# Token order of the last block, and stores of 32 rows, in a linear-attention and softplus-MLP kernel

## The chip, the cores and the metric

The kernel runs on one core of a Trainium2 chip. The core has a matrix engine (TensorE, PE; its weight loads are shown apart as PEld), a vector engine (VectorE, DVE), a scalar engine (ScalarE, ACT), a general engine (GpSimd, POOL) and a synchronisation engine (SyncE, SP), which in this kernel issues all the large DMAs. The metric is the time on the device for one execution, in microseconds (us). A profile is one execution; its span runs from the first to the last instruction.

## What is computed

Two blocks follow each other. The first is a linear attention with a normalised output, for 8 batches of 8 heads, 576 tokens and 64 features:

```python
kv = einsum('bhsd,bhse->bhde', k, v)
o  = einsum('bhsd,bhde->bhse', q, kv)
x  = o / sqrt(mean(o*o, axis=-1) + 1e-6) * g_norm
```

Its result is turned into 4608 tokens of 512 features, and the second block is

```python
h   = x @ w_in            # 512 -> 2048
out = softplus(h) @ w_out # 2048 -> 512
```

The result is 4608 rows of 512 float32 numbers, a row being 2 KB.

## The kernel before

**Tiles, blocks and phases.** The tokens are cut into 36 tiles of 128 (P), t = 0 to 35, and these into 12 blocks of three tiles (TB = 3), n = 0 to 11. The 2048 hidden features are 16 chunks of 128. One step is one chunk for one block: 12 matmuls of w_in against the block's x (L658, 384 tokens wide), softplus on ACT (L678), a split of its result into three terms that together keep the precision (L680 on ACT, L669 and L673 on DVE), and 9 matmuls of those against w_out (L665). The weights of all chunks don't fit, so the chunks are worked in three phases; the sums of a phase are written to DRAM (part) and added in the next (L703 loads them, L705 adds on DVE). In the last phase L705 makes the output rows in a tile ot, and a store on SP takes them to out.

**x on its way.** The attention makes x of a tile on DVE (L535), while steps of earlier blocks run on PE. The matmuls want x with features as rows, so it must be turned. Tiles 0 to 11 are turned by PE (BY_PE = 12, L540) and stored to a DRAM buffer xd[n] of 512 features by 384 tokens. From tile 12 on DVE does it in blocks of 32 x 32 (L615), into a tile xb that holds three tiles, a block's worth. The ring xb has one place. When the third tile is in, four DMAs (L619), one for each group a of 32 partitions, store it to xd[n]. In xb the 32 tokens of group a of the three tiles lie beside each other, so the stores write runs of 3 x 32 = 96 tokens (384 B), and the tokens of a block stand in xd[n] in the order (group a, tile, token in the group) and not in their own. The steps don't care for the order of tokens. x_of(t) then reads back 128 consecutive columns (L636), which are four groups of 32 tokens that come from different tiles. x_there[t] holds the stores that this load waits for.

**Results put back in order.** For tiles from 12 on the rows of a result tile are thus four groups of 32 rows, each of which belongs to another place of out. Group m of tile i of the block is group a of the original tile u, with a, u = divmod(4 * i + m, 3). The store (L711 to L719) puts neighbouring groups with the same a into one DMA, whose destination is then k runs of 32 rows that lie 128 rows apart. For i = 0, 1, 2 this gives 3 + 1, 2 + 2 and 1 + 3 groups: two DMAs for a tile. Tiles 0 to 11 are stored by one DMA of 128 rows (L723, L724).

**What sets the order.** A planner (class Plan) gets every piece of work with an engine, an estimated time in ns, what it comes after, the places of rings that it takes and gives back, a position pos, and for DMAs a size in ns. It plays the run through and issues the program in the order that comes out. On each engine that order is fixed: an instruction that waits holds all behind it. A task that needs a ring's place is put where the planner expects the place to be free; a real semaphore wait guards it on the chip. For a DMA task the place comes free at the planner's own DMA time plus 2000 ns. Result tiles come from rings m (13 places) and x (2 places).

Of the kernel before, what the change touches and what calls it, by code (L numbers as in the profile page):

```python
# [18 lines left out]
P = 128  # L19
# [21 lines left out]
class Plan:  # L41
# [13 lines left out]
    def slot(self, ring):  # L55
        return Slot(ring)

    def add(self, engine, ns, run, after=(), pos=0.0, take=(), give=(), size=0, behind=None, follows=None):
        t = Task(engine, ns, run, [a for a in after if a is not None], pos, list(take), list(give), size)
        for s in t.give:  # L60
            s.readers += 1
        self.tasks.append(t)
        t.follows = follows
        t.behind = behind
        return t
# [77 lines left out]
def kernel(  # L143
# [24 lines left out]
    nc = tc.nc  # L168
    B, H, S, D = q.shape
    d_model, d_ff = moe_w_in.shape  # L170
# [4 lines left out]
    NT = 384  # L175
    TB = NT // P
    n_blocks = n_tokens // NT
    n_tiles = n_tokens // P
# [5 lines left out]
    LAST = PHASES[-1]  # L184
# [5 lines left out]
    BY_PE = 12  # L190
# [27 lines left out]
    slot, add = plan.slot, plan.add  # L218

    def new(s, shape, dtype=F32):  # L220
        pool = ps if s.ring in PS else sb
        s.tile = pool.tile(shape, dtype, tag=f"{s.ring}_{s.place}", name=f"{s.ring}_{s.place}")
        return s.tile
# [164 lines left out]
    def parts(t):  # L388

        b, s0 = divmod(t * P, S)  # L390
        if s0 + P <= S:
            return [(b, 0, P, s0)]
        return [(b, 0, S - s0, s0), (b + 1, S - s0, P - S + s0, 0)]

    first_tile = [b * S // P for b in range(B)]
    xd = [dram.tile([d_model, NT], F32, name=f"x{n}") for n in range(n_blocks)]
# [5 lines left out]
    BL = 32  # L402
# [57 lines left out]
    def x_pos(t):  # L460

        n = t // TB
        return t * EARLY[0] + EARLY[1] if n == 0 else first_step[0, n] - (EARLY[2] if n == 1 else EARLY[3]) + t % TB
# [52 lines left out]
    def rows(t):  # L516
        pos = x_pos(t)
# [24 lines left out]
        def part_of_qT(n, r0):  # L542
            if qT.tile is None:
                new(qT, [P, NP, P])
            return qT.tile[:, :, r0:r0 + n]

        turned = []
        for b, r0, n, s0 in parts(t):
            if b >= 2:
                if b not in q_slots:  # L550
# [3 lines left out]
                        out=part_of_qT(n, r0),  # L554
                        in_=q_slots[b].tile.rearrange("k (p s) -> k p s", p=NP)[:, :, s0:s0 + n]),
# [28 lines left out]
            a = add("PE", 440, turn_q, [ld], pos - 1, [tp], [q_s])  # L584
# [3 lines left out]
        a = o_task = add("PE", 830 if len(parts(t)) == 1 else 1350, out_rows, turned + need, pos, [o], [qT])  # L588
        for pt in parts(t):
            o_tasks.setdefault(pt[0], []).append(a)  # L590
        a = add("ACT", 600, lambda: nc.scalar.activation(new(x, [P, H, D]), o.tile, func=AF.Square,  # L591
                                                              scale=D ** -0.5), [a], pos, [x])
        a = add("DVE", 690, reduce, [a], pos, [r])
        a = add("POOL", 2300, root, [a], pos)
        a = add("DVE", 700, norm, [a, o_task], pos, [], [o, r])
        if t < BY_PE:
            a = add("PE", 440, turn_x, [a], pos + 0.5, [xp], [x])
            if t < AT_ONCE:
                split(0, t, xp, a, pos + 0.5)
            a = add("ACT", 600, lambda: nc.scalar.copy(new(xg, [P, KD, P]), xp.tile), [a], pos + 1, [xg], [xp])  # L600
            x_there[t] = [add("SP", 450, lambda: nc.sync.dma_start(
                out=x_of(t), in_=xg.tile), [a], pos + 1, [], [xg], 1000)]
# [2 lines left out]


        n, i = divmod(t, TB)
        if i == 0:
            xb_slots[n] = slot("xb"), []
        xb, turns = xb_slots[n]  # L610

        def turn_blocks():
            if i == 0:
                new(xb, [P, d_model // BL, TB, BL])
            nc.vector.transpose(out=xb.tile[:, :, i], in_=x.tile.rearrange("p h d -> p (h d)").rearrange(  # L615
                "p (b j) -> p b j", j=BL))

        def store(a):
            nc.sync.dma_start(out=xd[n][:, a * TB * BL:(a + 1) * TB * BL].rearrange("(b i) m -> i b m", i=BL),  # L619
                              in_=xb.tile[a * BL:(a + 1) * BL].rearrange("i b t j -> i b (t j)"))  # L620

        turns.append(add("DVE", 710, turn_blocks, [a], pos, [] if i else [xb], [x], follows=turns[-1] if i else None))
        if i == TB - 1:
            stores = [add("SP", 450, lambda a=a: store(a), turns, pos + 0.5, [], [xb], 820) for a in range(P // BL)]
            for u in range(n * TB, t + 1):
                x_there[u] = stores

    def x_of(t):

        n, i = divmod(t, TB)  # L630
        return xd[n][:, i * P:(i + 1) * P].rearrange("(a p) t -> p a t", p=P)
# [9 lines left out]
    part = {}  # L641
# [3 lines left out]
    def step(s):  # L645
# [38 lines left out]
        for i in range(TB):  # L684
            last = c == cs[-1]
            a2 = add("PE", 700, lambda i=i: mm2(i), [a] + factors_done[1, c] + [mm2s.get(i)], s + 1.5,
                     [mine[i]] if c == cs[0] else [],
                     [gv] + ([w_out] if s == last_step[c] else []))
            mm2s[i] = a2
            if last:  # L690
                leave(ph, n * TB + i, mine[i], a2, s + 1.5)
# [3 lines left out]
    def leave(ph, t, bank, done, pos):  # L695

        ot = slot("m" if ph == 0 else ("m", "x", "m")[t % TB] if ph == LAST else "m")
        if ph == 0:
            a = add("ACT", 600, lambda: nc.scalar.activation(new(ot, [P, d_model]), bank.tile, func=AF.Copy, scale=1.0 + E),
                    [done], pos, [ot], [bank])  # L700
        else:
            pt = slot("m")
            ld = add("SP", 350, lambda: nc.sync.dma_start(out=new(pt, [P, d_model]), in_=part[ph - 1, t][0]),  # L703
                     [part[ph - 1, t][1]], pos - EARLY[10], [pt], [], 900, behind=int(pos) - 4)
            a = add("DVE", 700, lambda: nc.vector.scalar_tensor_tensor(  # L705
                out=new(ot, [P, d_model]), in0=bank.tile, scalar=(scale if ph == LAST else 1.0 + E), in1=pt.tile,
                op0=ALU.mult, op1=ALU.add), [done, ld] + (scale_done if ph == LAST else []), pos, [ot], [bank, pt])
        if ph == LAST and t >= BY_PE:
            n, i = divmod(t, TB)

            def store():  # L711
                m = 0
                while m < P // BL:
                    a, u = divmod(P // BL * i + m, TB)
                    k = min(TB - u, P // BL - m)
                    nc.sync.dma_start(
                        out=out[n * NT:(n + 1) * NT].rearrange("(t s) f -> t s f", t=TB)[u:u + k, a * BL:(a + 1) * BL],
                        in_=ot.tile[m * BL:(m + k) * BL])
                    m += k  # L719

            part[ph, t] = None, add("SP", 800, store, [a], pos, [], [ot], 750)
            return
        dst = out[t * P:(t + 1) * P] if ph == LAST else dram.tile([P, d_model], F32, name=f"part{ph}_{t}")  # L723
        st = add("SP", 350, lambda: nc.sync.dma_start(out=dst, in_=ot.tile), [a], pos, [], [ot], 720)  # L724
        part[ph, t] = dst, st
# [28 lines left out]
    for c in range(KF):  # L754
        for j in (2 * c, 2 * c + 1):
            pos = CONVERT[j] if c < 4 else LATER[c - 4] + LATER[12] * (j % 2)
            weight(j, pos, FETCH[j] if c < 4 else pos)
    for b in range(B):
        kv_of(b)
        for t in range(n_tiles):  # L760
            if parts(t)[-1][0] == b:
                rows(t)
# [51 lines left out]
```

## Time and profile before

| what | value |
|---|---|
| median of three timed runs | 934.63 us (933.73 to 934.82) |
| the profiled run, timed | 934.44 us |
| span of its profile | 932.7 us |
| DMA, mean over the span | 141 GB/s |
| stores of results, L716 | 48: 16 of 192 KB, 16 of 128 KB, 16 of 64 KB |
| stores of results, L724 to out | 12 of 256 KB |
| stores of x from xb, L619 | 32 of 192 KB |

In lines of the profile an operation is named by engine, line and operation; out<-in are the tiles that it writes and reads. The row of an issue on SP (SPq) shows only the time that issuing took, not when the data landed. In a table of stretches, each row has the stretch, its length, the busy time and number of instructions for PE, PEld, DVE, ACT and POOL, the clock granted to PE, the busy share of the 16 DMA engines and what they moved in GB/s. In the row of DMA a digit is the share of the engines that is busy in a column, in tenths.

### The profile page before, as it was taken

To read this page: it belongs to the slowest core of one execution; us is meant where nothing else is said; L and a number is where in the kernel's file an instruction comes from. 1 tells how busy PE (TensorE), PEld (TensorE's weight loads), DVE (VectorE), ACT (ScalarE), POOL (GpSimd) and SP (SyncE) were. 2 spreads that over 40 slices of the span, in tenths; PEclk is the share of its full clock that TensorE was granted. 3 is DMA by queue.
4 is the path that set the end of the run, shared out by engine and by line. 5 is a ranking of instruction groups with operands and counts; after the bars stand their busy time and mean duration, and the time that the engine had idled before them with its cause. 6 is when DMAs were issued, how large, how long until landed. Compare 5 with 4: busy or idle time off the path is not lost.

```text
span 932.7 us, 13257 instructions
## 1 busy us (share of the span) xinstructions
PE 904.9 (97%) x4821; PEld 818.5 (88%) x4821; DVE 627.3 (67%) x1055; ACT 414.5 (44%) x799; POOL 80.4 (9%) x78
## 2 busy tenths in 40 slices
PE   7899999999999999999999999999999999999992
PEld 5689899989999999999999999989999998999992
DVE  6777788776458887788757878887434455655531
ACT  4766555444433656464424455555322323333320
POOL 0323421221113100000000000000000000000000
PEclk8999999999999999999999999999999999999997
DMA  8999998498782554346334445551231233444321
GB/s 213 225 225 222 248 212 205 102 212 151 171 143 90 147 147 136 112 145 206 102 102 128 148 157 169 189 182 39 85 102 56 81 102 102 106 119 127 109 75 42
DMA packets 231377, 131.43 MB, mean 141 GB/s; under 512 B 130448, under 2 KB 205200, under 8 KB 231312
## 3 DMA queue, kind: packets, MB, share of 16 engines
q1 hardware_dynamic: 231152, 130.58, 53.3%
q8 instruction: 38, 0.62, 0.3%
q14 instruction: 27, 0.22, 0.1%
q10 hardware_dynamic: 160, 0.00, 0.0%
HBM read 91.75 MB, written 38.80 MB: 140 GB/s over the span
## 4 chain that ended last, share of the span: by engine, by line
PE 93%; SPq 2%; DVE 1%; DMA 1%; POOL 1%; ACT 1%; issue 0%; ACTq 0%
PE s L665 43%; PE h L658 43%; PE o L523 3%; PE o L506 3%; SPq L568 1%; DMA g_col<-in_g_norm_dram 1%; PE tp L540 0%; POOL r L532 0%; DMA m<-in_v_dram 0%; DMA qa<-in_q_dram 0%; DVE m L312 0%; PE tp L578 0%; DVE r L528 0%; DVE xv L440 0%; DVE m L316 0%
## 5 line engine op out<-in xcount | busy, mean ns | idle before, releaser
L658 PE MATMUL h<-xv,w 128*128 128x384 f32 x2304 | 434.6, 337 | 0.0
L665 PE MATMUL s<-w,gv 128*128 128x512 f32 x1728 | 434.3, 395 | 0.0
L658 PEld LDWEIGHTS h<-xv,w 128*128 128x128 f32 x2304 | 406.2, 188 | 14.8 <-issue 0.2
L665 PEld LDWEIGHTS s<-w,gv 128*128 128x128 f32 x1728 | 319.5, 188 | 59.1 <-issue 0.5
L678 ACT ACTIVATE g<-h 128x384 f32<-128x384 f32 x192 | 94.3, 491 | 398.4 <-PE h L658 394.4
L669 DVE TENSOR_TENSOR gv<-g,gv 128x384 fp32r<-128x384 f32 x192 | 106.6, 555 | 175.9 <-ACT gv L680 175.0
L680 ACT ACTIVATE gv<-g 128x384 fp32r<-128x384 f32 x192 | 100.9, 525 | 23.3 <-PE s L665 16.6
L673 DVE SCALAR_TENSOR_TENSOR gv<-gv 128x384 fp32r<-128x384 f32 x192 | 107.0, 557 | 6.0
L440 DVE SCALAR_TENSOR_TENSOR xv<-m,g_col,xv 128x512 fp32r<-128x512 f32 x102 | 75.8, 743 | 1.1 <-ACT xv L437 1.1
L444 DVE SCALAR_TENSOR_TENSOR xv<-xv 128x512 fp32r<-128x512 f32 x108 | 74.5, 690 | 2.6
L437 ACT ACTIVATE xv<-m,g_down 128x512 fp32r<-128x512 f32 x102 | 69.7, 710 | 2.5 <-DMA m<-x 2.4
L532 POOL TENSOR_TENSOR r<-r,half 128x8 f32<-128x8 f32 x36 | 65.8, 1826 | 3.0
L506 PEld LDWEIGHTS o<-m,m 128*128 128x128 f32 x256 | 34.2, 200 | 8.7 <-issue 7.3
L506 PE MATMUL o<-m,m 128*128 128x128 f32 x256 | 35.4, 285 | 6.4 <-DMA m<-in_v_dram 6.4
L705 DVE SCALAR_TENSOR_TENSOR m<-s,scale,m 128x512 f32<-128x512 f32 x24 | 17.9, 747 | 29.7 <-PE s L665 29.7
L523 PE MATMUL o<-kv_diag,m 128*128 128x128 f32 (+1 forms) x296 | 36.9, 275 | 0.0
L523 PEld LDWEIGHTS o<-kv_diag,m 128*128 128x128 f32 (+1 forms) x296 | 35.0, 179 | 1.8 <-issue 1.0
L531 POOL TENSOR_SCALAR r<-r 128x8 f32<-128x8 f32 x36 | 13.9, 386 | 244.9 <-DVE r L528 244.8
L535 DVE TENSOR_TENSOR x<-o,r 128x512 f32<-128x512 f32 x33 | 22.7, 688 | 17.6 <-POOL r L532 17.6
L528 DVE TENSOR_REDUCE r<-x 128x8 f32<-128x512 f32 x36 | 24.5, 681 | 13.3 <-ACT x L591 13.2
L705 DVE SCALAR_TENSOR_TENSOR m<-s,m 128x512 f32<-128x512 f32 x36 | 23.3, 684 | 10.2 <-PE s L665 10.1
L286 ACT ACTIVATE sq<-raw 128x512 bf16<-128x512 bf16 x32 | 21.3, 665 | 16.4 <-DMA raw<-in_moe_w_in_dram 10.2
(67 smaller groups left out, 445.6 us busy)
## 6 DMA issues: line engine op xcount, KB each, us to landing
m<-x SPq DMA_DIRECT2D x102, 256.0 KB
part<-m SPq DMA_DIRECT2D x72, 256.0 KB
m<-part SPq DMA_DIRECT2D x72, 256.0 KB
raw<-in_moe_w_in_dram SPq DMA_DIRECT2D x16, 512.0 KB
m<-in_k_dram SPq DMA_DIRECT2D x64, 128.0 KB
m<-in_v_dram SPq DMA_DIRECT2D x32, 256.0 KB
raw<-in_moe_w_out_dram SPq DMA_DIRECT2D x16, 512.0 KB
qa<-in_q_dram SPq DMA_DIRECT2D x24, 288.0 KB
```

The lines of the kernel that those rows point to most:

```text
L437: nc.scalar.activation(cols(0, F32R), x.tile, func=AF.Identity, scale=g_down)
L440: nc.vector.scalar_tensor_tensor(out=cols(1, F32R), in0=x.tile, scalar=g_col, in1=cols(0), op0=ALU.mult, op1=ALU.subtract)
L444: nc.vector.scalar_tensor_tensor(out=cols(2, F32R), in0=cols(1), scalar=-RADIX, in1=cols(0), op0=ALU.mult, op1=ALU.add)
L506: nc.tensor.matmul(kv[:, i if tail else p], lhsT=l, rhs=r, start=(p == 0 and i == 0), stop=tail, skip_group_check=True)
L523: nc.tensor.matmul(y[r0:r0 + n, p::NP], lhsT=qT.tile[:, p, r0:r0 + n], rhs=kv_diag[b % 2][:, p].rearrange("r (h d) -> r h d", d=D), start= ...
L532: nc.gpsimd.tensor_tensor(out=r.tile, in0=r.tile, in1=half, op=ALU.pow)
L658: nc.tensor.matmul(hp, lhsT=w_in.tile[:, i, kd * P:(kd + 1) * P], rhs=xv.tile[:, i, kd], start=(m == 0), stop=(m == 3 * KD - 1))
L665: nc.tensor.matmul(mine[i].tile, lhsT=gv.tile[:, m, i * P:(i + 1) * P], rhs=w_out.tile[:, m], start=(c == cs[0] and m == 0), stop=(c == cs ...
L669: nc.vector.tensor_tensor(out=gv.tile[:, 1], in0=g.tile, in1=gv.tile.bitcast(F32)[:, 0], op=ALU.subtract)
L673: nc.vector.scalar_tensor_tensor(out=gv.tile[:, 2], in0=f32[:, 1], scalar=-RADIX, in1=f32[:, 0], op0=ALU.mult, op1=ALU.add)
L678: a = add("ACT", 490, lambda: nc.scalar.activation(new(g, [P, NT]), h.tile, func=AF.Softplus, scale=1.0 + E), [a], s, [g], [h])
L680: a = add("ACT", 530, lambda: nc.scalar.activation(new(gv, [P, 3, NT], F32R)[:, 0], g.tile, func=AF.Copy, scale=DOWN), [a], s, [gv])
```

## The change

There are two parts.

The last block (n = 11, tiles 33, 34 and 35) keeps its tokens in order. A group size g is 3 for the other blocks and 1 for the last: each of its tiles takes an xb of its own, is turned into it, and is stored by four DMAs, whose runs are 32 tokens (128 B) instead of 96. A tile's read-back then waits for its own stores alone. As its tokens are in order, its results leave by the plain path, L723 and L724, one DMA of 128 rows for each tile.

The other tiles from 12 on (12 to 32) store their results by four DMAs of 32 rows, one for each group, whose destinations are each contiguous, in place of two whose destinations have up to three runs. The planner's time for the four is 1600 ns instead of 800, and its size for a store of the last block's x is 490 instead of 820.

```diff
         n, i = divmod(t, TB)
+        g = TB if n < n_blocks - 1 else 1
+        i0, i = i - i % g, i % g
         if i == 0:
             xb_slots[n] = slot("xb"), []
...
-                new(xb, [P, d_model // BL, TB, BL])
+                new(xb, [P, d_model // BL, g, BL])
...
-            nc.sync.dma_start(out=xd[n][:, a * TB * BL:(a + 1) * TB * BL].rearrange("(b i) m -> i b m", i=BL),
+            nc.sync.dma_start(out=xd[n][:, i0 * P + a * g * BL:i0 * P + (a + 1) * g * BL].rearrange("(b i) m -> i b m", i=BL),
...
-        if i == TB - 1:
-            stores = [add("SP", 450, lambda a=a: store(a), turns, pos + 0.5, [], [xb], 820) for a in range(P // BL)]
-            for u in range(n * TB, t + 1):
+        if i == g - 1:
+            stores = [add("SP", 450, lambda a=a: store(a), turns, pos + 0.5, [], [xb], 820 if g > 1 else 490)
+                      for a in range(P // BL)]
+            for u in range(t - i, t + 1):
                 x_there[u] = stores
...
-        if ph == LAST and t >= BY_PE:
+        if ph == LAST and BY_PE <= t < n_tiles - TB:
             n, i = divmod(t, TB)
 
             def store():
-                m = 0
-                while m < P // BL:
+                for m in range(P // BL):
                     a, u = divmod(P // BL * i + m, TB)
-                    k = min(TB - u, P // BL - m)
-                    nc.sync.dma_start(
-                        out=out[n * NT:(n + 1) * NT].rearrange("(t s) f -> t s f", t=TB)[u:u + k, a * BL:(a + 1) * BL],
-                        in_=ot.tile[m * BL:(m + k) * BL])
-                    m += k
-
-            part[ph, t] = None, add("SP", 800, store, [a], pos, [], [ot], 750)
+                    row = n * NT + u * P + a * BL
+                    nc.sync.dma_start(out=out[row:row + BL], in_=ot.tile[m * BL:(m + 1) * BL])
+
+            part[ph, t] = None, add("SP", 1600, store, [a], pos, [], [ot], 750)
             return
```

## The prediction

> **What bounds the kernel now.** I read the engine shares first, then a table of stretches, then the end of the timeline, then the DMA columns there. The page's first line:
>
> ```profile
> PE 904.9 (97%) x4821; PEld 818.5 (88%) x4821; DVE 627.3 (67%) x1055; ACT 414.5 (44%) x799; POOL 80.4 (9%) x78
> ```
>
> TensorE (PE) is the bound. A mean hides where its missing 3% lies, so the table of stretches (start:end, length, busy time of each engine, clock, DMA share, GB/s) is next:
>
> ```profile
> 0.00:50.00 50.00, 39.93 (x229) 31.58 (x230) 35.28 (x63) 30.28 (x59) 9.93 (x14) 0.93 0.87 215
> ...
> 300.00:345.00 45.00, 45.00 (x238) 41.01 (x237) 37.77 (x66) 27.10 (x55) 7.49 (x7) 1.00 0.54 149
> ...
> 771.00:896.00 125.00, 125.00 (x629) 113.35 (x628) 69.19 (x114) 40.98 (x78) 0.00 (x0) 1.00 0.38 108
> 896.00:916.30 20.30, 20.26 (x100) 17.57 (x98) 8.95 (x15) 4.47 (x9) 0.00 (x0) 1.00 0.28 78
> 916.30:932.70 16.40, 0.00 (x0) 0.00 (x0) 0.75 (x2) 0.00 (x0) 0.00 (x0) 0.59 0.21 48
> ```
>
> From 100 us to 916.3 us PE has no idle stretch: there, moving a DMA can only do harm or nothing. But 16.4 us at the end hold no matmul at all. What lies there, from the timeline (start, length):
>
> ```profile
> 914.91 0.75 DVE L705 SCALAR_TENSOR_TENSOR m<-s,scale,m 128x512 f32<-128x512 f32 x1 [0.59 <-PE s L665]
> 915.61 0.75 DVE L705 SCALAR_TENSOR_TENSOR x<-s,scale,m 128x512 f32<-128x512 f32 x1
> 915.69 1.21 SPq L716 DMA_DIRECT2D out_dram<-m  x2
> 916.30 0.75 DVE L705 SCALAR_TENSOR_TENSOR m<-s,scale,m 128x512 f32<-128x512 f32 x1
> 917.01 1.53 SPq L716 DMA_DIRECT2D out_dram<-x  x2
> 918.64 1.29 SPq L716 DMA_DIRECT2D out_dram<-m  x2
> ```
>
> The last result (tile 35) is ready at 917.05, its second store is issued by 919.93. SP's waits for the stretch from 905 us on say what follows:
>
> ```profile
> SPq L809 <- DMA out_dram<-m: 11.6, 1, 11.6
> ```
>
> The drain at L809 waits 11.6 us for the last stores. Why so long for 768 KB? The DMA columns of 912 to 933 us (40 columns of 0.525 us; tenths busy over 16 engines, then GB/s):
>
> ```profile
> DMA  1100000000492332234221111111111111100000
> GB/s 47 47 12 0 0 0 0 0 0 23 39 78 51 70 105 86 51 55 94 78 59 51 51 39 27 35 47 55 47 55 51 51 55 47 55 31 16 0 0 0
> ```
>
> The stores crawl at about 50 GB/s with a tenth of the engines busy: in 924 to 928 us the stretch reads share 0.13 and 44 GB/s, so 0.13 x 16 = 2 engines at 21 GB/s each. The last data is at column 35, about 930.6; the span ends 2.1 us later. The same 768 KB from a block whose tokens are in order (tiles 0 to 2, L724), 648 to 660 us in columns of 0.3 us:
>
> ```profile
> DMA  0000000006980009949985799999869999898651
> GB/s 0 0 0 0 0 0 0 0 0 239 348 287 0 0 0 341 375 150 348 314 285 121 205 309 295 341 336 306 258 205 239 304 278 355 335 382 341 266 198 61
> ```
>
> One 256 KB store, issued at 649.97, fills columns 9 to 11, (239 + 348 + 287) x 0.3 = 262 KB in 0.9 us, from 650.7: 16 engines.
>
> **What the Trainium skill says.** "DMA: Bandwidth & Descriptors", section "Why a DMA increments its semaphore by 16 and not by 1": the number of engines is the largest up to 16 that divides the slowest dimension, size-1 ones apart, of both access patterns. For a destination of 3 x 32 rows that is 3, for 2 x 32 rows 2, for 32 or 128 rows 16, always the lowest-numbered ones. The trace agrees: per tile L716 issues 3+1, 2+2, 1+3 groups of 32 rows, so the last three tiles give engines 0 and 1 each 64 x 4 = 256 KB and engine 2 128 KB; 256 KB at 21 GB/s is 12.5 us. The same page, "Anatomy of one DMA", gives some 2 us of fixed cost, most of it the write's receipt; the 2.1 us after the last column agree. Its "Specifications" want runs of 512 B for line rate; the trace's 384-byte runs (x<-xb, L619) go at about 170 GB/s, the q loads' 128-byte runs at about 138 GB/s with engines full, the 2 KB stores above at 350.
>
> **The change part by part.**
>
> *Last block's results (tiles 33 to 35): six L716 issues out, three L724 stores of 128 rows in.* Issue: a plain L724 store takes 0.34 us. Results are ready at 915.66, 916.36, 917.05 (DVE is untouched), so the third is issued at about 917.1; its data starts 0.75 us later (649.97 to 650.7), 917.85. The three transfers need 3 x 0.9 us from 915.69 + 0.75 = 916.45 at the earliest, so the second ends near 918.1 and the third at 919.0. With 2.1 us to the end: 921.1; with the receipt a little shorter in an idle machine, down to 920.6. I take 920.9. Against 932.7: **11.8 us saved**, all of it on the path that sets the end.
>
> *Tiles 12 to 32: four stores of 32 rows, 64 KB each, instead of two.* 42 issues become 84. Each of the old pair has a median of 0.59 to 0.74 us; the new one is two-dimensional like L724 (0.34), so a tile costs SP 1.4 us at best and 4 x 0.59 = 2.4 at worst against 1.2, for three tiles of a block of 20.9 us 0.6 to 3.6 us more. Queued behind them on SP are the loads of partial sums (L703) and of x (L636). Those of the last block are issued at 862.71 to 868.56 and first read by ACT at 879.55, so 11 us of slack hide the delay. There is a gain too that nobody waits for: L636's three loads take 5.8 us to issue behind a store on few engines, 1.5 us elsewhere. On the path: nothing, since PE is full from 771 to 916.
>
> *Last block's x (rows 33 to 35, 310 to 337 us): three times four stores of 64 KB in runs of 128 B instead of four of 192 KB in runs of 384 B.* SP: 8 issues more x 0.70 us (2.82 us per four at 331.40) = 5.6 us, into SP's idle stretches of 312.25 to 320.38 and 320.72 to 331.40; hidden. DMA: 2048 pieces of 384 B at 170 GB/s cost 4.6 us; now 6144 of 128 B, at 138 GB/s 5.7 us; were a piece as dear as a 384-byte one, 13.8 us. DMA's share there is 0.54, and the block's x is read back at 337.23 for steps that begin at 358: hidden. What is not clearly hidden is a **new wait**. Ring xb has one place, so each tile's block transpose (L615) must wait till the stores of the tile before have landed. DVE then:
>
> ```profile
> 311.93 0.71 DVE L615 STREAM_TRANSPOSE xb<-x 128x512 f32<-128x512 f32 x1
> ...
> 314.37 0.56 DVE L669 TENSOR_TENSOR gv<-g,gv 128x384 fp32r<-128x384 f32 x1 [0.55 <-ACT gv L680]
> 314.96 0.56 DVE L673 SCALAR_TENSOR_TENSOR gv<-gv 128x384 fp32r<-128x384 f32 x1
> ...
> 316.04 0.70 DVE L615 STREAM_TRANSPOSE xb<-x 128x512 f32<-128x512 f32 x1
> ```
>
> Tile 34's transpose at 316.04 moves back. Tile 33's stores can be issued from 312.7 to 315.5, behind 2 MB that the columns show flowing until 316.4. Their data (256 KB) takes 1.9 to 4.6 us, the receipt 2: landed between 318.5 (nothing ahead) and 323. The planner puts the transpose where it believes the place free, with 4 x 490 ns for these data where I have 1.9 to 4.6 us, 1.8 us of issues where the trace has 2.8, 6.96 us for the transfers ahead where it shows 7.7. So DVE may stand at it 0.7 to 4.3 us. Behind it in order stand L669 and L673, whose output PE reads 1.75 us after it is ready (315.52, the matmul at 317.27). PE can lose 0 to 2.6 us, once: tile 35 comes 14 us later. A gain is excluded, since PE is full there. I take 0.4, nearer the low end, as the planner may leave L669 ahead of the transpose.
>
> *Sum against the profiled span*: 932.7 - 11.8 + 0.4 = 921.3. The three timed runs (median 934.63) stand 1.9 us above this span: **923.2 us**.
>
> **Rivals.** (1) The forecast, 921.8 to 924.3: 0.70. (2) The tail goes, but the new wait costs PE 1.5 to 4 us: 924.3 to 926.8, at 0.14. For it: DVE is 84% busy from 300 to 345 us. Against: the planner knows the wait. (3) The tail goes only in part, say because three stores that arrive together make the write receipt slow, 3 to 6 us more: 926 to 929, at 0.06. Against it: 16 engines ran at 350 GB/s at 650 us. (4) Slower. A 128-byte write to HBM could cost far more than the 128-byte read that the trace shows. Place: tile 34's transpose, with all of DVE and then PE held behind it. Each ns of packet cost is 128 packets per engine and tile = 0.13 us; the 11.8 us are eaten once stores land some 13.5 us (with the 1.75 of slack) after the plan's 2 us of data, about 120 ns a packet, against 36 for one of 384 B. At 150 ns a tile's data takes 19 us, the loss is 15, and the time 938: 0.05. (5) The store's tail turns out to be bound by the end of the program and not by the stores, which leaves 934.6, no change: 0.05 with all other ways to nothing; the columns, which show data till 930.6, speak against it.
>
> **How the numbers follow.** A measurement tells 0.2%, 1.9 us, from no change. Faster: 0.70 + 0.14 + 0.06 = 0.90, and part of (5) makes 0.91; same 0.03; slower 0.06 with mishaps of (2) beyond its end. The low end is the forecast less 0.3 us of the receipt and 1.1 us of the spread of the runs, 921.8; the high end takes in most of (2): 926.5.
>
> **What would show it.** After the change the last columns should read 250 to 350 GB/s for 3 us, SP's final wait should fall from 11.6 to about 3.5 us, and the last matmul should still end near 916.3. A last matmul later than 918, with DVE idle before L615 near 318 us, would be (2); beyond 928, (4). It is wrong if the three stores still land at 50 GB/s.

## The result

| kernel | median, us | runs | span of its profile, us |
|---|---|---|---|
| before | 934.66 | 933.73 to 934.82, 4 | 932.7 |
| changed | 922.49 | 922.42 to 922.67, 4 | 920.4 |

The changed kernel takes 0.9871 of the time before, with an interval of 0.9855 to 0.9887: 12.2 us less, where 11.5 had been forecast (923.2 us, range 921.8 to 926.5).

**Where the time came from.** The table of stretches of the changed kernel (start:end, length, busy PE, PEld, DVE, ACT, POOL, clock, DMA share, GB/s), to be held against the one of before:

```profile
300.00:345.00 45.00, 45.00 (x238) 41.01 (x237) 37.95 (x67) 28.00 (x56) 7.74 (x7) 1.00 0.58 152
...
771.00:896.00 125.00, 125.00 (x629) 113.35 (x628) 69.45 (x114) 41.01 (x78) 0.00 (x0) 1.00 0.37 108
896.00:916.30 20.30, 20.30 (x101) 17.78 (x99) 8.69 (x15) 4.69 (x10) 0.00 (x0) 1.00 0.27 78
916.30:920.40 4.10, 0.22 (x1) 0.00 (x0) 1.01 (x2) 0.00 (x0) 0.00 (x0) 1.00 0.51 192
```

PE is as full as it was up to its last matmul. The stretch after that is 4.1 us and not 16.4, and DMA runs in it at 192 GB/s on the mean and not at 48. The timeline of the end (start, length):

```profile
915.17 0.75 DVE L708 SCALAR_TENSOR_TENSOR m<-s,scale,m 128x512 f32<-128x512 f32 x1 [0.59 <-PE s L668]
915.87 0.75 DVE L708 SCALAR_TENSOR_TENSOR x<-s,scale,m 128x512 f32<-128x512 f32 x1
915.95 0.35 SPq L723 DMA_DIRECT2D out_dram<-m  x1
916.56 0.75 DVE L708 SCALAR_TENSOR_TENSOR m<-s,scale,m 128x512 f32<-128x512 f32 x1
916.65 0.35 SPq L723 DMA_DIRECT2D out_dram<-x  x1
917.34 0.33 SPq L723 DMA_DIRECT2D out_dram<-m  x1
```

Each result is issued within 0.1 us of its end, in one DMA. SP's wait at the end, and the DMA columns of 912 to 921 us (0.225 us each):

```profile
SPq L808 <- DMA out_dram<-m: 1.7, 1, 1.7
```

```profile
DMA  0000000000000000000006999999996000000000
GB/s 0 0 0 0 0 0 0 0 0 0 0 0 0 0 0 0 0 0 0 0 0 237 400 355 346 382 373 401 355 400 246 0 0 0 0 0 0 0 0 0
```

The three stores flow one behind the other at 350 to 400 GB/s, from 916.7 to 919.0; there the share of the 16 engines that is busy is 0.92. From the last result (917.31) to the end of the span it is 3.05 us; in the kernel before it was 932.66 - 917.05 = 15.61 us. The difference, 12.56 us, is a little more than the whole gain of the spans (12.3): the changed kernel's profile reached its last result 0.26 us later, and that shift is there already at 300 us (the block transpose of tile 33 starts at 312.19, before at 311.93), ahead of all that the change touches.

**The new wait.** DVE around the last block's x:

```profile
312.19 0.71 DVE L617 STREAM_TRANSPOSE xb<-x 128x512 f32<-128x512 f32 x1
...
319.40 0.56 DVE L676 SCALAR_TENSOR_TENSOR gv<-gv 128x384 fp32r<-128x384 f32 x1
319.88 0.70 DVE L617 STREAM_TRANSPOSE xb<-x 128x512 f32<-128x512 f32 x1
```

The transpose of tile 34 moved from 316.04 to 319.88 and starts with no idle time before it: by then the stores of tile 33 had landed.

### The profile page after: what moved, and what is told of

The parts are those of the page before. It is cut to its first block, busy times and chain, and to the rows that moved or that the text cites. A ratio compares the mean times of both kernels' runs of the same rounds, so it can differ in the third digit from the quotient of the medians.

```text
span 920.4 us, 13312 instructions
## 1 busy us (share of the span) xinstructions
PE 906.3 (98%) x4821; PEld 819.5 (89%) x4821; DVE 626.8 (68%) x1055; ACT 414.5 (45%) x799; POOL 80.1 (9%) x78
## 4 chain that ended last, share of the span: by engine, by line
PE 95%; DVE 1%; DMA 1%; SPq 1%; ACT 1%; issue 0%; POOL 0%; ACTq 0%; DVEq 0%
PE s L668 44%; PE h L661 43%; PE o L506 4%; PE o L523 3%; SPq L568 1%; DMA g_col<-in_g_norm_dram 1%; PE tp L540 0%; PE h L777 0%; DMA m<-in_v_dram 0%; POOL r L532 0%; DVE m L312 0%; PE h L367 0%; PE tp L578 0%; DVE m L316 0%; DVE m L299 0%
## 5 line engine op out<-in xcount | busy, mean ns | idle before, releaser
L708 DVE SCALAR_TENSOR_TENSOR m<-s,scale,m 128x512 f32<-128x512 f32 x24 | 17.9, 746 | 29.7 <-PE s L668 29.7
L535 DVE TENSOR_TENSOR x<-o,r 128x512 f32<-128x512 f32 x33 | 22.7, 687 | 17.6 <-POOL r L532 17.6
L708 DVE SCALAR_TENSOR_TENSOR m<-s,m 128x512 f32<-128x512 f32 x36 | 23.3, 683 | 10.2 <-PE s L668 10.1
```

## The experiments

The theory: what ended the run was the number of DMA engines that the last block's stores got; all else in the change costs and brings nothing. The rivals: the order of the rows and where they lie in DRAM; the size and number of the DMAs; the stores of the middle tiles.

Two numbers are used below. The time tells what the change is worth. The *tail*, from the end of the last result's DVE instruction (L705 or L708) to the end of the span in one trace, is sharper, as the first 75 us of this kernel differ from one execution to the next: PE is busy between 20.2 and 22.6 us of the stretch from 25 to 50 us, in traces of kernels that have the same instructions there. The timed runs of one kernel spread by up to 3.2 us, which this may explain.

### The token order alone

The kernel before with the first part of the change: tiles 12 to 32 keep their two DMAs on few engines. Besides the new x stores of the last block:

```diff
-        if ph == LAST and t >= BY_PE:
+        if ph == LAST and BY_PE <= t < n_tiles - TB:
```

> Theory (few engines at the end): the last block's results leave on 16 engines, as in the changed kernel, and the middle tiles' stores on few engines are hidden behind a full PE, so 922.5 us, within 0.5 of the changed kernel. Rival (the middle stores hold back loads that matter): 923.5 or more.

Measured: 921.75 us (921.33 to 923.7), ratio 0.9862 (0.9849 to 0.9876), tail 3.03 us. That is the whole gain. The median lies 0.7 us under the one of the changed kernel, less than its own four runs are apart, so no difference from it can be told.

### The middle stores alone

The kernel before, with one group in each DMA for tiles 12 to 32 (and the planner's 1600 ns for them, as in the change).

```diff
-                    k = min(TB - u, P // BL - m)
+                    k = 1 if t < n_tiles - TB else min(TB - u, P // BL - m)
```

> Four 32-row DMAs for tiles 12 to 32, the last block as before. Theory: PE is full there, so 934.7, no change. Rival (the middle stores are part of the gain): 933 or less.

Measured: 935.01 us (13 runs), ratio 1.0001 (0.9993 to 1.001), tail 15.29 us. This part of the change is worth nothing in time. Yet it does what it was expected to do on SP. After the third tile's store of a block SP issues the next loads of x; in the timeline of the run with the token order alone, which stores the middle tiles as before (first fence), and in that of this run (second):

```profile
859.61 3.02 SPq L719 DMA_DIRECT2D out_dram<-m  x2
862.73 5.86 SPq L639 DMA_DIRECT2D m<-x  x3
```

```profile
862.37 1.78 SPq L716 DMA_DIRECT2D out_dram<-m  x4
864.25 1.53 SPq L636 DMA_DIRECT2D m<-x  x3
```

For the third tile of a block, which these lines show, four issues take 1.8 us where two took 3.0, and the three loads behind them 1.5 where they took 5.9. For the first two tiles it is the other way round: four issues take 1.7 to 1.8 us and two took 1.2 to 1.3. On balance SP is freed, but nobody was waiting for it.

### Groups of 32 rows for all tiles, the tokens as before

The kernel before with the second part of the change, for tiles 33 to 35 too.

```diff
         if ph == LAST and t >= BY_PE:
...
-                while m < P // BL:
+                for m in range(P // BL):
                     a, u = divmod(P // BL * i + m, TB)
...
+                    row = n * NT + u * P + a * BL
+                    nc.sync.dma_start(out=out[row:row + BL], in_=ot.tile[m * BL:(m + 1) * BL])
```

> Token order of the last block as before, all tiles from 12 on stored by four 32-row DMAs. Theory: the crawl goes, since each DMA has 16 engines; what is left is SP's issuing, 12 issues of 0.44 us from 915.95 on, the last begun at 920.8 and landed 1.7 us later: span 922.8, time 924.9. Rival (scattered rows of the unordered tokens are slow to write, so the order is what matters): 932 to 935.

Measured: 925.76 us (924.75 to 926.83), ratio 0.9901 (0.9886 to 0.9916), tail 6.48 us. Rows that go to the very places of before, out of order, gain 9.2 us (934.92 less 925.76), three quarters of what the change gains, as soon as each DMA has a destination of 32 rows. The rival of scattered rows falls. What is left is issuing. The end of this kernel, timeline and then the columns of 914 to 934 us (0.5 us each):

```profile
916.06 1.72 SPq L715 DMA_DIRECT2D out_dram<-m  x4
916.67 0.75 DVE L705 SCALAR_TENSOR_TENSOR m<-s,scale,m 128x512 f32<-128x512 f32 x1
917.88 1.78 SPq L715 DMA_DIRECT2D out_dram<-x  x4
919.76 1.79 SPq L715 DMA_DIRECT2D out_dram<-m  x4
```

```profile
DMA  0000025755555555400000000000000000000000
GB/s 0 0 0 0 0 53 143 168 131 139 139 135 135 135 131 131 131 0 0 0 0 0 0 0 0 0 0 0 0 0 0 0 0 0 0 0 0 0 0 0
```

SP issues with gaps of only 0.1 us from 916.06 to 921.55, 0.43 us and more for 64 KB, and DMA moves no more than that, 135 GB/s at half its engines' time.

### The same, half of the last block's stores issued from ACT

Against the last kernel:

```diff
-                    nc.sync.dma_start(out=out[row:row + BL], in_=ot.tile[m * BL:(m + 1) * BL])
+                    queue = nc.scalar if t >= n_tiles - TB and m % 2 else nc.sync
+                    queue.dma_start(out=out[row:row + BL], in_=ot.tile[m * BL:(m + 1) * BL])
```

> As the run with groups only, but every other store of the last block is issued from ACT's queue. Theory (what is left there is SP's issuing): the issues end at 918.6 and not 921.2, so 922.3 to 923.0. If scattered rows were slower to write or to land: no better than the run with groups only.

Measured: 923.55 us (923.16 to 923.78), ratio 0.9882 (0.9867 to 0.9897), tail 4.14 us: 2.3 us of the 3.4 that the tail of the last kernel had over the change come back, and its columns rise from 135 to as much as 291 GB/s. The last issues of the two queues:

```profile
917.81 0.84 SPq L716 DMA_DIRECT2D out_dram<-m  x2
918.01 0.79 ACTq L716 DMA_DIRECT2D out_dram<-m  x2
```

They end at 918.80, 1.44 us after the last result (917.36); in the changed kernel it is 0.36 us. These 1.1 us are as much as the tail still has over the one of the changed kernel, so nothing is left that the places of the rows would have to explain. The expectation was 0.6 to 1.3 us too low, the sum having ended with the landing (see below).

### The sizes of before, in order

The changed kernel, with two DMAs for each tile of the last block.

```diff
+        cut = (96, 64, 32)[t % TB]
...
+            for r0, r1 in ((0, cut), (cut, P)):
+                nc.sync.dma_start(out=dst[r0:r1], in_=ot.tile[r0:r1])
```

> The changed kernel, but each tile of the last block leaves in two DMAs of 96 + 32, 64 + 64 and 32 + 96 rows, the sizes that the kernel before has, with destinations in order. Theory: 96, 64 and 32 all divide by 16, so 16 engines, one issue of some 0.4 us more: 922.5 to 923.2. Rival (sizes and number of the DMAs made the tail): 930 or more.

Measured: 925.79 us (924.48 to 926.29), ratio 0.9899 (0.9886 to 0.9913), tail 4.82 us. The number missed by some 2.6 us at the least. The tail accounts for 1.8 us of the distance to the changed kernel: the pairs of issues took 0.79, 1.20 and 1.00 us, so the last DMA was issued about 1.4 us after the last result (917.4 to 920.2 is the range of their starts), where the forecast had 0.4, and the data flowed at no more than 250 GB/s between the issues. The rest lies ahead of the end (last result at 918.78, in the changed kernel at 917.31), in the first 75 us; after that PE is full in both. It is still 10.8 us shorter in its tail than the kernel before with DMAs of the same sizes in the same sequence. Sizes and number are thus not what made the tail; what differs at the end is the shape of the destination, 96 rows in one piece and not 3 x 32, and with it the order of the rows, which the runs with groups have dealt with.

### The engines taken away again

The decisive run: contiguous rows, in order, but 124 and 4 of them.

```diff
+        cut = 124
...
+            for r0, r1 in ((0, cut), (cut, P)):
+                nc.sync.dma_start(out=dst[r0:r1], in_=ot.tile[r0:r1])
```

> The changed kernel, but each tile of the last block leaves in DMAs of 124 and of 4 rows, in order and contiguous. Theory (engines by divisor): 124 and 4 have 4 as the largest divisor up to 16, so engines 0 to 3 have 3 x 64 = 192 KB each, 9.4 us at 21 GB/s from 916.7: span 927.6, time 929.7. Rival (order and places of rows): 922.5 to 923.2.

Measured: 930.48 us (929.56 to 930.84), ratio 0.9955 (0.994 to 0.997), tail 10.63 us. Order and places are those of the changed kernel, there is one more DMA per tile, and the crawl is back. Its columns, 914 to 934 us:

```profile
DMA  0000002312222222222222221000000000000000
GB/s 0 0 0 0 0 0 49 29 16 66 61 74 102 102 98 98 98 111 102 98 98 106 102 78 53 29 0 0 0 0 0 0 0 0 0 0 0 0 0 0
```

From 920 to 924 us the share is 0.26 and the rate 101 GB/s: 4 of 16 engines at 25 GB/s.

### Only some of the last three tiles

Two kernels of before in which only tiles 33 and 34, or only tile 35, leave in groups of 32 rows (and have the planner's 1600 ns for it).

```diff
-                    k = min(TB - u, P // BL - m)
+                    k = 1 if t in (33, 34) else min(TB - u, P // BL - m)
```

In the other kernel the condition is t == 35.

> The kernel before, but tiles 33 and 34 leave in groups of 32 rows; tile 35 as before (32 rows, then 3 x 32). Theory: only the last 192 KB runs on 3 engines, 64 KB each at 21 GB/s = 3.1 us from 920.7, landed 1.5 us later: span 925.4, time 927.5. Rival (rows in token order are what counts): 933 to 935.

Measured: 928.72 us (928.31 to 928.93), ratio 0.9937 (0.9922 to 0.9952), tail 9.32 us; the forecast counts on the times of the changed kernel's trace, and its span less the last result there, 917.3, makes 8.1.

> The kernel before, but tile 35 alone leaves in groups of 32 rows. Theory: engine 0 still has 64 + 4 KB of tile 33, 128 of tile 34 and 16 of tile 35 = 212 KB, 10.3 us at 21 GB/s from 916.7: span 928.5, time 930.6. If only the last transfer's own shape counted: 924 to 925.

Measured: 932.52 us (930.5 to 933.71, 20 runs), ratio 0.9974 (0.9967 to 0.9981), tail 12.89 us; the forecast makes 11.2. The last transfer's own shape is not what counts: with tile 35 on 16 engines most of the tail stays. That its shares on engines 0 and 1 stand behind those of tiles 33 and 34 would explain it.

Both are longer than forecast. With the run of 124 rows they give the load of the busiest engine against the tail. The load is worked out by the rule that the prediction took from the Trainium skill ("DMA: Bandwidth & Descriptors", section "Why a DMA increments its semaphore by 16 and not by 1"): the largest number of engines up to 16 that divides the slowest dimension of both sides, always the lowest-numbered ones. No view here shows a single engine; what the runs show is that the tail grows with this load:

| kernel | on engine 0, KB | tail, us |
|---|---|---|
| changed | 48 | 3.05 |
| 124 + 4 rows | 192 | 10.63 |
| tile 35 alone in groups | 212 | 12.89 |
| before | 264 | 15.61 |

A straight line from the first to the last is (15.61 - 3.05) / (264 - 48) = 0.058 us for a KB, an estimate of 17.6 GB/s for one engine, idle time between its shares counted in. It gives 11.4 and 12.6 us for the two in the middle. The run with tiles 33 and 34 in groups (100 KB) isn't in the table, as its last pair of DMAs is issued only from 920.04 on and SP's issuing is a part of its tail. The same goes for the runs with groups only, two queues and the sizes of before (48 KB each, tails of 4.14 to 6.48 us).

### The x stores three times

The changed kernel, with each store of the last block's x made thrice, twice of it into spare buffers.

```diff
+    twins = [dram.tile([d_model, NT], F32, name=f"twin{i}") for i in range(2)]
...
+            for twin in (twins if g == 1 else []):
+                nc.sync.dma_start(out=twin[:, i0 * P + a * g * BL:i0 * P + (a + 1) * g * BL].rearrange("(b i) m -> i b m", i=BL),
+                                  in_=xb.tile[a * BL:(a + 1) * BL].rearrange("i b t j -> i b (t j)"))
```

> The changed kernel, but each store of the last block's x (rows 33 to 35, runs of 128 B) is made three times, two of them to spare DRAM buffers; the planner isn't told. The place of xb comes free later: 12 issues of 0.5 us from 312.9 on, landed near 322, and the transpose of tile 34, planned at 319.9, waits some 2 us. Theory (the new wait has slack, DVE 2 us and PE 1.75 us): PE loses 0 to 1 us, 922.5 to 923.5. Rival (the wait passes on to PE at once): 925 to 928.

Measured: 922.61 us (922.47 to 922.77), ratio 0.9868 (0.9852 to 0.9885), tail 3.12 us. The wait is there now, as DVE's timeline shows:

```profile
319.87 0.56 DVE L680 SCALAR_TENSOR_TENSOR gv<-gv 128x384 fp32r<-128x384 f32 x1
321.61 0.71 DVE L618 STREAM_TRANSPOSE xb<-x 128x512 f32<-128x512 f32 x1 [1.18 <-DMA twin<-xb]
```

DVE stands 1.18 us, and PE loses nothing: it is busy for 45.00 of the 45 us from 300 to 345. So three times as many of the narrow stores could be made, and the end of the run would not see it.

## Why the prediction was right

**The end of the kernel** was the right place, and the mechanism was right: most of the 768 KB lay on two engines, some 260 KB on each. That it is the engines and not the rows was only read from the Trainium skill's rule and the columns then; the runs of groups only and of 124 rows show it from both sides.

**The sum of the tail** was 0.8 us too long: 920.9 - 917.05 = 3.85 us against 3.05. The term that was mis-sized most is the time from the last data to the end: the prediction read 2.1 us and took 1.9, and the changed kernel has 1.4. Its reading of the trace of before was too long. It put the last data into column 35, at 930.6, but the column after it, which begins at 930.9, still shows 16 GB/s, and in columns of 0.1 us the last data stands at 931.1, 1.5 us before the end. Nor is this time one receipt of a write. SP's wait of 11.6 us from 919.93 on ends at 931.5, some 0.4 us after the last data, and 1.1 us follow in which no store is waited for. In the changed kernel a 256 KB store lands 2.0 us after its issue begins, at about 919.4, again 0.4 us after the last data, and the program then needs 1.0 us more to its last instruction. The other term was the data: predicted to flow until 1.95 us after the last result, measured 1.66, as stores that follow each other run at up to 400 GB/s and not at the mean of 290 that one store alone showed. The 1.0 us after the landing is what the expectations with a landing time in them (groups only, two queues, tiles 33 and 34) left out: each was about 1 us short. SP's final wait was forecast at 3.5 us and is 1.7, as the forecast counted it to the end of the span.

**The new wait** was costed at 0.4 us, from 0 to 2.6, and is nothing. The step that was off is "behind 2 MB": the planner put the stores of tile 33 ahead of a weight load of 512 KB, so less stood in front of them. SP in the kernel before (first fence) and in the changed one (second):

```profile
311.75 0.50 SPq L275 DMA_DIRECT2D raw<-in_moe_w_in_dram  x1
```

```profile
312.93 2.04 SPq L621 DMA_DIRECT2D x<-xb  x4
315.02 0.55 SPq L275 DMA_DIRECT2D raw<-in_moe_w_in_dram  x1
```

The four stores of tile 33 landed 2.8 to 3.2 us after their issues, of which the last began at 314.4, so by about 317.6. That is before the early end of the bound (318.5), and the transpose of tile 34 stood at 319.88.

**Sum**: 921.3 - 0.8 - 0.4 + 0.26 for the later start is the span of 920.4; the timed median stands 2.1 us above it, not 1.9. The 0.26 and the 0.2 us are chance; they hide a part of the 1.2 us by which the two terms were too long, so that the time is only 0.7 us off.

**The middle tiles at nothing**: shown by the run that does this part alone. The four issues of most tiles took 1.75 to 1.8 us (one set took 2.9), in the bound of 1.4 to 2.4. That a block would cost SP 0.6 to 3.6 us more did not come true: the 1.2 us that were counted for an old pair hold for the first two tiles of a block, and the third tile's pair took 3.1. Together the stores of the block at 855 us took SP 5.5 us before and 5.3 after the change.

**Rivals.** A tail that goes only in part did not come. Nor did a slower kernel by dear 128-byte writes: even three times as many of them cost no time. What the prediction did not ask is how much of its gain needs the tokens in order: some 3 us of 12.2 (925.76 against 922.49), 2.3 of which a second issuing queue takes off the tail, and 1.1 are the later end of the issues that is left. So in the tail they are what twelve issues at the end cost over three, not the places of the rows.

## What to carry to other kernels

When a kernel ends in a wait for its stores, look at the DMA columns there: a steady low share with little data moving (here 0.13 for two engines, 0.26 for four) can be a transfer on few engines. In these runs the outermost dimension of the destination made the difference: stores of 3 x 32, 2 x 32 and 124 rows crawled, and stores of 32, 64, 96 and 128 rows in one piece, all multiples of 16, did not. Give it a multiple of 16; where that needs more DMAs, count their issues, as after the last result nothing hides them. In the middle of such a kernel the same cure is worth nothing while the bound engine is full.

## What had not been expected

Transfers on few engines hold up the queue that issues them. The prediction had read the two figures, 5.8 and 1.5 us for three loads, from different places of one trace; the run with the middle stores alone shows that the shape of the store before them decides: in the five blocks from 771 to 870 us they took 1.5 to 2.1 us, where they took 5.8 to 6.0 behind the old stores. Why the issuing stops is not shown; no run looked at it. A DMA of 32 rows costs SP 0.42 us (median), more than one of 128 rows at 0.34. And from the landing of the last store to the end of the span there is about 1 us (1.1 before, 1.0 in the changed kernel, 1.1 with groups only), which no change of the stores in these runs moved.
